# Sparse attention with a chosen expert: a rebuilt first batch, another list order, and products of a constant tile in TensorE's waits

## The chip, the cores and the metric

The kernel runs on one core of a Trainium2 chip. The metric is the device time of one execution in microseconds (us); lower is better. A core's engines are TensorE (PE in the profile, its weight loads PEld), VectorE (DVE), ScalarE (ACT), GpSimd (POOL) and SyncE (SP). The last two mostly issue transfers here. Every kernel below was checked against the reference, and all were correct.

## The reference

Four batches of 768 positions, 8 heads of 64. Each position attends to the 15 neighbours on either side and to 24 blocks of 32 positions (maximum of k, mean of v). The mean over the attention output chooses one of eight experts for the whole batch, and the batch then goes through that expert alone.

```python
k_sum = k.reshape(B, H, nb, block, D).max(axis=3)
v_sum = v.reshape(B, H, nb, block, D).mean(axis=3)
...   # softmax over [scores inside the window, scores on blocks + log(32)]
attn = np.matmul(a, np.concatenate([v, v_sum], axis=2))
...
pooled = x.mean(axis=1)
e_idx = np.argmax(pooled @ w_gate, axis=1)
h = np.maximum(x[mask] @ w1[e], 0.0)
out[mask] = gate_w[mask, None, None] * (h @ w2[e])
```

So an expert's weights can't be fetched before the last attention product of its batch has gone through the gate.

## The kernel before

A small list scheduler in the kernel's source estimates durations, orders all operations of all batches, and emits each engine's list in that order. Each engine then works through its list in order. The parts that matter:

```python
# three expert banks in PSUM, each a tile of its own
mps_pool = ctx.enter_context(tc.tile_pool(name="mps", bufs=3, space=PS))
...
def mm():                                   # one expert group: 4 products into one bank
    sb["hps"] = mps_pool.tile([128, 512], FP32, name="hps")
    for dt in range(NDT):
        nc.tensor.matmul(sb["hps"][:, 0 : c1 - c0], lhsT=..., rhs=..., start=(dt == 0), stop=(dt == NDT - 1))
def rl():                                   # ScalarE evicts it
    nc.scalar.activation(sb["hT"][:, ft, c0:c1], ps["t"][:, 0 : c1 - c0], ACT.Relu)
```

```python
def halo_v(b, hs):        # neighbour rows of v, copied inside the chip
    vb = vblks[b % 2]
    if b > 0:             # batch 0 loads these 16 rows from memory instead
        nc.sync.dma_start(vb[0:16, 1:NJ, hs, :], vb[64:80, 0 : NJ - 1, hs, :])
    nc.sync.dma_start(vb[80:96, 0 : NJ - 1, hs, :], vb[16:32, 1:NJ, hs, :])
...
for j in range(NJ):       # block sums of v, read from rows 0 to 79
    nc.tensor.matmul(ps[0:32, 0 : n * D], lhsT=bind[:, j, :], rhs=vblks[b % 2][0:80, j, hs, 0:D], ...)
...                       # then VectorE copies them out and SyncE broadcasts them into rows 96 to 119
for hh in range(2):       # probabilities times v: 12 products of 120 rows
    for jj in range(NH):
        nc.tensor.matmul(ops[...], lhsT=aT[0:NR, hh, ...], rhs=vb[0:NR, j, 2 * pr + hh, :], start=True, stop=True)
```

Two one-column copies on GpSimd ("tokens"), which wait for loads of v, hold back the later loads of q and k.

The softmax here doesn't subtract the row's maximum and nothing guards it: scores larger than these inputs give would overflow.

## Time and profile before

| | before |
|---|---|
| time, median of 3 runs | 198.6 us (198.41 to 201.48) |
| gate product of batch 0, 1, 2, 3 | 43.8, 77.5, 121.7, 159.8 us |
| first expert product | 59.2 us |
| last expert product ends | 196.0 us |
| eviction, store and end | 3.8 us |

The rows split the span into stages. From 59.2 to 196.0 us TensorE is busy 124 of 136.8 us. Before that, the time is set by when the first gate product can run. The lines that show this stand in the prediction.

### The profile page before, as it was taken

Reading aid. Unit: us, or ns where it says so; the run is one execution under the profiler, and the core shown is the slowest. Engines: PE = TensorE matmul, PEld = TensorE weight load, DVE = VectorE, ACT = ScalarE, POOL = GpSimd, SP = SyncE. Lnnn points to the kernel's source line nnn. Section 1 sums busy time; section 2 is a strip of 40 time slices with the busy share of each in tenths; the row PEclk is TensorE's granted clock in tenths of the full one; section 3 lists DMA queues with packets and bytes.
Section 4 is the critical chain, followed back from the end, with each engine's and each line's share of the span. In section 5 each row is a group of like instructions: output and inputs, shape, how many; then the busy total and the mean of one; then the engine's idle time right before and its main releaser. Section 6 shows DMA issues by size and latency. Waiting matters only on the chain.

```text
span 199.8 us, 4547 instructions
## 1 busy us (share of the span) xinstructions
PE 160.0 (80%) x1902; PEld 93.0 (47%) x1924; DVE 100.7 (50%) x209; ACT 95.7 (48%) x182; POOL 42.4 (21%) x67
## 2 busy tenths in 40 slices
PE   0342877765989799999999899958999995399992
PEld 0231666544365475434556454334556542156440
DVE  5472488599386789311898781563797210000000
ACT  2203267442057676513778736223888642056431
POOL 6126934007420520911025001100000030000000
PEclk9999999999999999999999999996999999579999
DMA  5999999915999999899999957799200039980142
GB/s 86 210 179 156 178 227 214 166 32 80 178 179 225 198 175 151 138 191 257 267 239 191 184 78 208 147 218 242 39 3 0 3 111 229 260 137 0 56 153 111
DMA packets 28689, 30.45 MB, mean 152 GB/s; under 512 B 9756, under 2 KB 22812, under 8 KB 28572
## 3 DMA queue, kind: packets, MB, share of 16 engines
q0 software_dynamic: 14800, 19.40, 59.6%
q1 hardware_dynamic: 13868, 10.75, 21.3%
q8 instruction: 15, 0.25, 0.5%
q14 instruction: 6, 0.05, 0.1%
HBM read 36.06 MB, written 6.29 MB: 212 GB/s over the span
## 4 chain that ended last, share of the span: by engine, by line
PE 55%; DMA 25%; DVE 6%; SPq 4%; issue 3%; ACT 3%; POOL 2%; POOLq 1%; ACTq 0%
PE hps L726 23%; PE hps L760 15%; DMA w_sb<-in_moe_w_dram 11%; DMA v_f<-in_v_dram 7%; DMA q_nat<-in_q_dram 4%; PE ops L359 4%; PE sc L464 4%; SPq L216 3%; PE ops L497 3%; DMA vblk<-vblk 2%; PE kps L407 2%; PE tps L521 2%; PE tps L432 2%; DVE kT L426 1%; DVE xs L511 1%
## 5 line engine op out<-in xcount | busy, mean ns | idle before, releaser
L726 PE MATMUL hps<-xT_b,w_sb 128*128 128x256 bf16 (+1 forms) x239 | 50.3, 343 | 9.3 <-DMA w_sb<-in_moe_w_dram 7.9
L760 PE MATMUL hps<-w_sb,hT_sb 128*128 128x512 bf16 x187 | 43.4, 380 | 0.3
L741 ACT ACTIVATE hT_sb<-hps 128x512 bf16<-128x512 f32 x64 | 29.8, 490 | 23.4 <-PE hps L726 22.5
L726 PEld LDWEIGHTS <-w_sb 128*128 128x128 bf16 x256 | 23.3, 102 | 24.1 <-DMA w_sb<-in_moe_w_dram 7.9
L475 ACT ACTIVATE aT<-sc 128x768 bf16<-128x768 f32 x32 | 25.9, 809 | 15.7 <-PE sc L464 15.6
L770 ACT ACTIVATE o_sb<-hps,gcol 128x512 f32<-128x512 f32 x24 | 16.5, 687 | 28.2 <-PE hps L760 16.4
L760 PEld LDWEIGHTS <-hT_sb 128*128 128x128 bf16 x192 | 18.0, 98 | 20.5 <-issue 0.9
L213 POOL DMA_DIRECT2D v_f<-in_v_dram x24 | 18.0, 761 | 36.4 <-DMA w_sb<-in_moe_w_dram 26.0
L359 PE MATMUL ops<-vblk,bind 80*32 80x512 bf16 (+1 forms) x60 | 16.3, 445 | 6.0 <-DVE vblk L299 6.0
L479 DVE TENSOR_TENSOR aT<-aT,mask 120x768 bf16<-120x768 bf16 x32 | 17.6, 552 | 4.6 <-ACT aT L475 4.4
L426 DVE COPY kT<-kps 128x1152 bf16<-128x1152 bf16 x12 | 16.2, 1349 | 6.3 <-PE kps L407 6.3
L665 POOL DMA_DIRECT2D w_sb<-in_moe_w_dram x5 | 3.8, 753 | 72.3 <-PE hps L760 51.4
L299 DVE CAST vblk<-v_f 80x1536 bf16<-80x1536 f32 x16 | 14.9, 951 | 7.7 <-DMA v_f<-in_v_dram 7.7
L511 DVE TENSOR_TENSOR xs<-ops,rv 128x384 bf16<-128x384 f32 x32 | 17.8, 558 | 1.1
L407 PE MATMUL kps<-identb,k_nat 96*64 96x96 bf16 x256 | 11.3, 249 | 8.5 <-DMA k_nat<-in_k_dram 7.2
L497 PE MATMUL ops<-vblk,aT 120*64 120x65 bf16 x384 | 13.7, 211 | 4.9 <-DVE xs L511 2.0
L529 ACT ACTIVATE xT_b<-tps 128x768 bf16<-128x768 bf16 x16 | 12.9, 809 | 8.9 <-PE tps L521 8.8
L497 PEld LDWEIGHTS <-aT 120*64 120x64 bf16 x384 | 10.0, 122 | 12.9 <-issue 5.0
L464 PE MATMUL sc<-qT,kT 64*128 64x64 bf16 x384 | 13.1, 210 | 2.9 <-ACT kT L456 1.2
L446 DVE TENSOR_REDUCE kmx<-kT 128x24 bf16<-128x768 bf16 x16 | 15.2, 948 | 0.1
L407 PEld LDWEIGHTS <-k_nat 96*64 96x64 bf16 x256 | 9.2, 139 | 10.6 <-DMA k_nat<-in_k_dram 7.2
L464 PEld LDWEIGHTS <-kT 64*128 64x128 bf16 x384 | 9.2, 105 | 10.0 <-issue 6.4
(55 smaller groups left out, 113.8 us busy)
## 6 DMA issues: line engine op xcount, KB each, us to landing
w_sb<-in_moe_w_dram POOLq DMA_DIRECT2D x7, 1024.0 KB, 15.8
out_dram<-o_sb SPq DMA_DIRECT2D x24, 256.0 KB, 5.1
v_f<-in_v_dram POOLq DMA_DIRECT2D x24, 192.0 KB, 11.2
k_nat<-in_k_dram POOLq DMA_DIRECT2D x6, 384.0 KB, 10.3
q_nat<-in_q_dram POOLq DMA_DIRECT2D x6, 384.0 KB, 11.3
v_f<-in_v_dram SPq DMA_DIRECT2D x7, 240.0 KB, 7.2
vblk<-vblk SPq DMA_DIRECT2D x6, 178.8 KB, 6.2
w_sb<-in_moe_w_dram POOLq DMA_DIRECT2D x2, 512.0 KB, 9.4
```

Source lines behind the costliest of these rows:

```text
L213: nc.gpsimd.dma_start(v_f[16:80, :, h, :], v[b, h].rearrange("(j p) d -> p j d", p=QB))
L359: nc.tensor.matmul(ps[0:32, 0 : n * D], lhsT=bind[:, j, :], rhs=vblks[b % 2][0:80, j, hs, 0:D], start=(j == 0), stop=(j == NJ - 1),)
L407: nc.tensor.transpose(kps[hh * D : (hh + 1) * D, g, 2 : 2 + SP], qk_nat[b][1][:, 2 * pr + hh, g, :], identb[0:SP, 0:SP],)
L426: nc.vector.tensor_copy(kdst, win)
L464: nc.tensor.matmul(sc[:, hh, jj * QB : (jj + 1) * QB], lhsT=sb["kT"][pr][rs, j, :], rhs=sb["qT"][pr][rs, j, :], start=True, stop=True, til ...
L475: nc.scalar.activation(aT, sb["sc"][:, :, 0 : NH * QB], ACT.Exp, scale=SCALE)
L479: nc.vector.tensor_tensor(out=aT[0:NR], in0=aT[0:NR], in1=mask[:, hf * NH : (hf + 1) * NH, :] .rearrange("p j c -> p (j c)") .unsqueeze(1) ...
L497: nc.tensor.matmul(ops[(j % 2) * QB : (j % 2 + 1) * QB, hh, jj // 2, :], lhsT=aT[0:NR, hh, jj * QB : (jj + 1) * QB], rhs=vb[0:NR, j, 2 * p ...
L511: nc.vector.tensor_tensor(out=sb["xs"][pr][:, hf * NS : (hf + 1) * NS, :, :].rearrange("p s h d -> p h s d"), in0=ops[:, :, :, 0:D], in1=r ...
L726: nc.tensor.matmul(sb["hps"][:, 0 : c1 - c0], lhsT=sb["w1"][:, dt, ft * 128 : (ft + 1) * 128], rhs=sb["xT"][:, dt, c0:c1], start=(dt == 0) ...
L741: nc.scalar.activation(sb["hT"][:, ft, c0:c1], ps["t"][:, 0 : c1 - c0], ACT.Relu)
L760: nc.tensor.matmul(ps["t"], lhsT=sb["hT"][:, ft, st * 128 : (st + 1) * 128], rhs=sb["w2"][:, ft, :], start=(ft == 0), stop=(ft == NFT - 1),)
```

## The change

Its intent: bring the first batch's data in earlier and in the order of need, drop the broadcast of its block sums, let the two halves of a head pair use different PSUM banks, keep TensorE's clock up by products of a constant tile in early and long waits, and order the list so that later batches' attention runs ahead of experts. Its core (set-up steps, estimated durations, the first batch's explicit sequence and a rule of the list scheduler, that a result of the same engine counts as ready once issued, are left out):

```diff
-    mps_pool = ctx.enter_context(tc.tile_pool(name="mps", bufs=3, space=PS))
+    mps_pool = ctx.enter_context(tc.tile_pool(name="mps", bufs=1, space=PS))
+    kbank = kps_pool.tile([128, 1024], BF16, name="kbank")     # k transposes, and a spare part
+    idle_ps = kbank[:, G * (SP + 4) : 1024].bitcast(FP32)
+    idle_in = const_pool.tile([128, 128], BF16, name="idle_in")
+    mps = mps_pool.tile([128, 3, 512], FP32, name="mps")
...
-        if b > 0:
-            nc.sync.dma_start(vb[0:16, 1:NJ, hs, :], vb[64:80, 0 : NJ - 1, hs, :])
+        nc.sync.dma_start(vb[0:16, 1:NJ, hs, :], vb[64:80, 0 : NJ - 1, hs, :])
...
-    tk = add("POOL", 0.2, [v_loads[2], bind_setup], lambda: nc.gpsimd.tensor_copy(tok[:, 0:1], ...))
...                      # tokens gone; v loads 2 to 7 on GpSimd's queue, between those of q and k
...
+            if second(pr, hf):                 # batch 0, second half of a pair
+                sc = mps[:, 0:2, :]
+            else:
+                sc = sc_pool.tile([128, 2, 512], FP32, name="sc")
...
+            if second(pr, hf):
+                ops = mps[:, 2, :]
...
+                    if b == 0 and jj % 2 == 1:    # block sums as an extra product of 24 rows
+                        nc.tensor.matmul(ops[:, hh, jj // 2, :], lhsT=aT[KW:NR, hh, (jj - 1) * QB : (jj + 1) * QB],
+                            rhs=vs0[KW:NR, 2 * pr + hh, :], start=False, stop=True, tile_position=(KW, 0))
...
-                sb["hps"] = mps_pool.tile([128, 512], FP32, name="hps")
+            ps = {"t": mps[:, len(sch.tags.get("mps", [])) % 3, :]}
...                      # list order
+    DELAY = {"PE": 0.9, "DVE": 0.6, "ACT": 0.6}
-                    elif (
-                        start + op["dur"] <= pick[0] + 0.1
-                        or (start < pick[0] and tail[pick[1]["n"]] - tail[op["n"]] < self.URGENT)
+                    elif start < pick[0] and (
+                        start + op["dur"] <= pick[0] + self.DELAY.get(eng, 0.1)
+                        or tail[pick[1]["n"]] - tail[op["n"]] < self.URGENT
-        sch.prio = 40.0 if b == 0 else 0.0
+        sch.prio = 40.0 if b == 0 else 8.0
...                      # constant products in planned waits
+                if t < self.FILL_TO:
+                    self.fill(int((idle - 0.4) / (0.1 if t < 8.0 else 0.08)))
+                else:
+                    self.fill(int((idle - 1.2) / 0.08))
+    def fill(n):
+        for _ in range(n):
+            nc.tensor.matmul(idle_ps, lhsT=idle_in, rhs=idle_in[:, 0 : idle_ps.shape[1]], start=True, stop=True)
```

## The prediction

> **What bounds the kernel now.** I read first the slices of the page, then the chain that ended last, then the same time cut into stages, then TensorE's own timeline. The slices of the kernel before:
>
> ```profile
> PE   0342877765989799999999899958999995399992
> PEclk9999999999999999999999999996999999579999
> DMA  5999999915999999899999957799200039980142
> ```
>
> One character is 5 us. TensorE is poorly filled for the first ten or eleven slices and nearly full from 60 us on, with two holes near 132 and 170 us. No other engine comes near this: VectorE is busy 50% and ScalarE 48% of the span. The stages (columns: stretch, its length, busy us and count on PE, weight loads, DVE, ACT, POOL, then clock, DMA share, GB/s):
>
> ```profile
> 7.20:43.90 36.70, 23.37 (x392) 17.85 (x392) 22.31 (x41) 15.60 (x24) 13.27 (x20) 1.00 1.05 172
> 43.90:59.20 15.30, 12.40 (x161) 7.86 (x161) 11.17 (x21) 3.96 (x8) 7.48 (x10) 1.00 0.88 133
> 59.20:132.70 73.50, 69.47 (x855) 38.39 (x868) 45.26 (x90) 41.81 (x85) 15.59 (x21) 1.00 1.01 191
> 132.70:135.40 2.70, 0.26 (x13) 0.23 (x8) 2.45 (x4) 0.64 (x1) 0.00 (x0) 1.00 1.12 189
> 135.40:167.50 32.10, 31.77 (x384) 17.13 (x388) 15.41 (x35) 20.34 (x41) 1.65 (x2) 0.95 0.35 78
> 167.50:172.90 5.40, 0.00 (x1) 0.00 (x0) 0.16 (x1) 0.69 (x1) 0.00 (x0) 0.76 1.09 243
> 172.90:196.00 23.10, 22.69 (x109) 11.50 (x112) 0.00 (x0) 10.51 (x21) 0.00 (x0) 0.91 0.40 100
> ```
>
> So there are three regimes. Up to 43.9 us (the first batch's attention, ending in its gate) no engine is full: a chain of small steps, held by loads, sets the time. From the gate to 59.2 us, the first expert product, the chosen expert's weights are fetched (issued at 46.15 us, first landing 8.5 us later at best). After 59.2 us TensorE is the bound, but for two waits in which the weights of batches 2 and 3 are not there. The chain of waits says the same:
>
> ```profile
> 13.01 4.94 DMA vblk<-vblk
> ...
> 124.18 10.97 DMA w_sb<-in_moe_w_dram
> ...
> 162.22 10.66 DMA w_sb<-in_moe_w_dram
> ```
>
> The first is the copy of the neighbour rows of v inside the chip; the others are the weight fetches, of which TensorE hides all but 2.46 and 5.43 us. Within the first stage the first product of probabilities and v starts at 24.3 us, though the first scores are exponentiated at 15.9: it waits for casts of v (which wait for v's load until 19.37), for neighbour rows, for block sums and, since TensorE's list is in order, for whatever stands before it. Finally TensorE's timeline:
>
> ```profile
> 49.60 5.30 PE L359 MATMUL ops<-vblk,bind 80*32 80x512 bf16 x12
> 58.35 0.50 PE L464 MATMUL sc<-qT,kT 64*128 64x64 bf16 x12
> 61.33 0.35 PE L464 MATMUL sc<-qT,kT 64*128 64x64 bf16 x12
> 126.39 2.81 PE L359 MATMUL ops<-vblk,bind 80*32 80x512 bf16 x12
> 172.93 0.61 PE L726 MATMUL hps<-xT_b,w_sb 128*128 128x512 bf16 x1 [5.43 <-DMA w_sb<-in_moe_w_dram]
> ```
>
> The same twelve block-sum products take 5.30 us early and 2.81 late. TensorE is slow from the start until about 61 us, although the clock row prints 9 there; that row cannot be trusted for the first 60 us, the durations can.
>
> **What the Trainium skill says.** "TensorE: Matmul & The Clock Gate", Part 1 (the HAM clock gate): the array starts at half clock, gets the full clock after some 3.4 us of activity and loses it after about as much idleness. The trace agrees: 5.30 against 2.81 us, and granted clock 0.76 in and 0.91 after the 5.4 us wait. The same page, Part 4 (PE-mode transpose), says transposes don't count as activity in the usual way. The trace fits: from 23 to 58 us TensorE was some three quarters busy with transposes, small attention products and 32-column block sums and never sped up; two microseconds of 128x128 expert products did it. So a filler of 128x128 weights is the right kind. "DMA: Bandwidth & Descriptors", Queues, rings and completion order: each DMA engine takes turns between the queues packet by packet. This fits the neighbour rows' 7.0 us to landing for 89 KB while v loads were running; I therefore don't count that copy as short after the change.
>
> **The change, part by part.**
>
> *Loads of the first batch.* The v loads are no longer 80 rows with 16 read twice, and only two of eight stay on the Sync queue; the rest follow on GpSimd's queue in the order of need, and GpSimd's two token waits (4.34 and 4.90 us) are gone. Issue costs about 0.75 us for a v load and 1.3 for a pair's q and k (GpSimd timeline), so six v loads, four pairs and the setup end near 1.5+6x0.75+4x1.3+3.0=14 us instead of 19 (last pair of the first batch issued at 18.0 to 19.3). The bytes as the profile counts them are 3.15 MB; at the observed 190 GB/s from 3.5 us that is 20 us, with neighbour rows and landing about 23 us (estimate).
>
> *Block sums.* Their broadcast into all blocks (146 KB twice, on the path at 35.8 us: 1.39 us of wait for it) is dropped for batch 0. Instead 3 extra products per head and half, 6 per group of 12: 48 in all, at about 25 to 45 ns (12 products take 0.31 to 0.54) under 2.2 us of TensorE, mostly in gaps.
>
> *Second PSUM set.* The second half of each pair uses expert banks that are idle then. Before, each product-normalise step took about 1.6 us (35.83, 37.49, 39.06, 40.73), one after another. Now it should come down toward VectorE's 0.75.
>
> *When is gate 0?* Three estimates. Data: last q and k at 23, then transposes 0.5, kT copy 1.13, maxima 0.95, spread 0.45, scores 0.3, exp 0.81, mask 0.56, product 0.5, normalise 0.75, half two 0.8, transpose 0.4, copy with sum 1.0: 8.15, with about 0.1 per hand-over 9.5, so 32.5. VectorE: first product near 18.5 (v cast 11, neighbour rows 7), then 8 normalisations 6.0, four masks 2.2, two pairs' copies and maxima 3.0, cast and sums 1.3 = 12.5, with some stalls 33. Second v group: cast near 20, rows 26.5, then four steps of 1 us and 1.7 for the end: 32. I take 33 against 43.9: 11 us.
>
> *Warm filler.* Warm, the first batch's TensorE groups fall from 0.85 to 0.5, 0.50 to 0.35, 0.54 to 0.38 us. About half lies on the path; this is inside the estimate. After the gate the 512-column block sums and seven transposes go warm (2.5 + 7x0.33 + some scores = about 5 us). If weights are issued at 33+2.4 and land after 8.5 to 9.5 us, the first expert product comes at 45 instead of 59.2: 14.2 us, of which 11 are the gate's and 3 the TensorE work that no longer stands in front.
>
> *List order.* Attention of later batches gets priority 8 us over the experts. At gate 3 (160 us) only 7.1 us of expert 2's products were left to cover the fetch of 10.7 (issue 2 us later), so 5.43 stayed open. Eight more microseconds held back cover that, and likewise the 2.46. I count 6 of 7.9, as an earlier attention also needs its own loads earlier. Filler and absence of waits save the half-speed start after each: the hidden products 172.93 to 185.42 take 12.5 where warm ones (32 of 0.216 and 32 of 0.135) would be 11.2, 1.3 us; about 1.5 at 135; say 2.8 together. Removed waits and cold starts do not overlap with anything but each other.
>
> Sum: 14.2+6+2.8=23; a further 1 for small waits in the list; 198.6-24=174.6. Check from the other side: 45 + (196.0-59.2-8-3.5) = 170.3 as last product, + 3.8 as before for eviction and store, + 1.5 (measured 201.35 against span 199.8) = 175.6, less a share of the profiled run's 2.8 us excess over the fast runs.
>
> **Rivals.**
> - *The DMA takes the place:* loads that came after the gate's idle patch (slice of 32 GB/s at 40 to 45 us) now crowd; batch 1's loads stand in GpSimd's queue before the first weights. For it: DMA share near 1.1 until 100 us. Against it: 112 to 123, 140 to 160 and 176 to 190 us are nearly empty. It would hold the first expert product near 52: 181 us.
> - *The filler doesn't warm, or gets in the way:* it runs before a real product in an in-order engine and is counted from planned gaps. Then gate 0 is at about 37 and the rest 3 us worse: 181 us.
> - *Weights waits stay* because attention cannot run ahead of VectorE's 26 us per batch (four pairs of 1.35+0.55+0.95+2x0.55+2x0.75, four casts of 0.95, sums 0.7): 180 us.
> - *Everything better:* gate near 29 and a tight list: 168 us.
>
> **Range and chances.** One rival alone gives 180 to 181, two 187. I predict 174.5, 167 to 183; faster by over 2% (under 194.6) 0.97.
>
> **What would show it.** Gate products at 33 (30 to 37) and first expert product at 45; score groups at 0.35 in the first 40 us, early 512-column block sums at 2.8; no TensorE wait over 1 us on weights of batches 2 and 3; from first expert product to last about 126 us. Wrong if the first weights land after 50, if early groups stay at 0.50, or if that last stretch remains 135.

## The result

| | before, same rounds | after |
|---|---|---|
| median of 5 runs | 201.48 us (198.41 to 210.71) | 248.4 us (244.32 to 249.17) |
| ratio of fast runs | | 1.232 (95%: 1.223 to 1.240) |
| gate products | 43.8, 77.5, 121.7, 159.8 us | 59.9, 114.3, 154.0, 191.1 us |
| first expert product | 59.2 us | 79.4 us |
| last expert product ends | 196.0 us | 242.5 us |

Ratios here and below are the mean time of one kernel's fast runs over that of the other's fast runs of the same rounds, so they are not quite the ratio of the medians. Executions over 1.5% slower than the fastest of the same kernel are left out of the means. Both profiled executions lay above their kernel's fast runs, by a similar share: 201.35 us (before, fast from 198.41) and 249.17 us (after, fast runs 243.88 to 245.27; the first of these is a sixth run, not among the median's five). So the stages are compared like with like.

The change was predicted to save 24 us and cost 46. By stages: up to the end of the first gate product 16.3 us more (60.2 against 43.9), from there to the first expert product 3.9 more (19.2 against 15.3), among the experts 26.4 more (163.2 against 136.8), and 0.5 at the end.

The slices of the page for the kernel after; one character is a fortieth of the span, here 6.2 us:

```profile
PE   5509989998679867999996798998798776655862
PEclk9965555555555897799999999999999999999999
DMA  6999891000699995015899999799200499100123
```

TensorE, poorly filled in the first 60 us before, is now full there from 20 us on. Its granted clock is at half for 60 us, and it is loosest (5 to 8) in the last 60 us, where before it had been nearly full apart from one wait for weights. The stages, in the columns of the prediction's stage table:

```profile
60.20:79.40 19.20, 15.09 (x173) 10.18 (x171) 11.13 (x20) 2.86 (x7) 7.49 (x10) 0.50 0.93 145
79.40:242.60 163.20, 131.03 (x1412) 69.37 (x1408) 65.21 (x130) 75.03 (x149) 17.20 (x23) 0.97 0.63 122
20.00:60.00 40.00, 38.22 (x453) 27.66 (x452) 17.53 (x36) 15.33 (x23) 4.32 (x6) 0.50 0.47 82
```

The last row is the reading that turns the case: from 20 to 60 us TensorE is busy 38.2 of 40 us at half clock, while the DMA engines idle half the time. Data is not what is missing; the array's own work is. The second row says the opposite of the expert stage: it is 32 us longer than TensorE's work in it, so there it waits. For what, is in TensorE's waits (columns: what waited for what; us in total, times, longest):

```profile
PE mps L837 <- ACT hT_sb L848: 18.0, 37, 0.7
PE ops L405 <- DMA vblk<-vblk: 7.9, 2, 6.7
PE mps L866 <- ACT o_sb L876: 7.4, 10, 0.8
...
PE kbank L949 <- DVE kT L476: 4.1, 2, 2.7
PE kbank L949 <- DVE kbank L248: 2.5, 1, 2.5
PE mps L837 <- ACT o_sb L876: 2.3, 3, 1.3
```

The first, third and last of these lines (with one more wait of 1.0 us of the same kind, 28.7 us together) are expert products that wait for ScalarE's evictions of the group before. In the kernel before no such wait appears: its expert products wait only for weights and, for 0.9 us, for issue. The second line is the block sums waiting for the neighbour rows; the fourth and fifth are constant products, which wait themselves and hold up what stands behind them. The chain that ended last, after (start, duration, what), shows the first kind in the row:

```profile
237.89 1.90 PE mps L866 x8
...
239.86 0.70 ACT o_sb L876
240.56 0.04 issue
240.60 1.90 PE mps L866 x8
```

Product group, eviction, product group: one output tile every 2.71 us (240.60 - 237.89), although three banks are rotated through. Before, the same stretch of TensorE's timeline is one unbroken row, 8 products in 1.79 us:

```profile
185.42 10.52 PE L760 MATMUL hps<-w_sb,hT_sb 128*128 128x512 bf16 x47
```

Finally TensorE's timeline after, to be read against the one in the prediction (start, length, line, tiles, count, and in brackets the idle time before):

```profile
2.53 4.27 PE L949 MATMUL kbank<-idle_in 128*128 128x112 bf16 x44 [2.53 <-DVE kbank L248]
6.72 0.55 PE L457 MATMUL kbank<-identb,k_nat 96*64 96x96 bf16 x16
...
18.92 2.51 PE L405 MATMUL ops<-vblk,bind 80*32 80x256 bf16 x11 [6.74 <-DMA vblk<-vblk]
21.36 0.85 PE L457 MATMUL kbank<-identb,k_nat 96*64 96x96 bf16 x16
...
28.76 0.27 PE L556 MATMUL mps<-vblk,aT 96*64 96x65 bf16 x2
28.96 0.23 PE L564 MATMUL mps<-vs,aT 24*128 24x65 bf16 x1
29.12 0.27 PE L556 MATMUL mps<-vblk,aT 96*64 96x65 bf16 x2
...
72.35 5.30 PE L405 MATMUL ops<-vblk,bind 80*32 80x512 bf16 x12
```

The constant products at 2.5 us do warm the array: the next 16 transposes take 0.55 us. Then the block sums wait 6.74 us for the neighbour rows, and from there the same transposes take 0.85. The products of probabilities and v come in trios of two and one, 0.36 us from one trio to the next (29.12 - 28.76), so a half takes six trios, 2.16 us. Before, at the same half clock, a half was:

```profile
24.32 0.53 PE L497 MATMUL ops<-vblk,aT 120*64 120x65 bf16 x12
```

And at 72 us the block sums of batch 1 still take the cold 5.30 us.

### The profile page after: what moved, and what is told of

Its sections match the earlier page's. It is cut to its first block, busy times and chain, and to the rows that moved or that the text cites. A ratio compares the mean times of both kernels' runs of the same rounds, so it can differ in the third digit from the quotient of the medians.

```text
span 246.9 us, 5000 instructions
## 1 busy us (share of the span) xinstructions
PE 192.8 (78%) x2146; PEld 114.8 (46%) x2146; DVE 103.7 (42%) x211; ACT 101.7 (41%) x185; POOL 46.0 (19%) x70
## 5 line engine op out<-in xcount | busy, mean ns | idle before, releaser
L837 PE MATMUL mps<-xT_b,w_sb 128*128 128x512 bf16 (+1 forms) x256 | 52.4, 338 | 20.5 <-ACT hT_sb L848 18.0
L866 PE MATMUL mps<-w_sb,hT_sb 128*128 128x512 bf16 x192 | 45.3, 379 | 8.4 <-ACT o_sb L876 7.4
L848 ACT ACTIVATE hT_sb<-mps 128x512 bf16<-128x512 f32 (+1 forms) x64 | 29.4, 489 | 41.9 <-PE mps L837 41.8
L876 ACT ACTIVATE o_sb<-mps,gcol 128x512 f32<-128x512 f32 x24 | 16.4, 687 | 41.3 <-PE mps L866 31.6
L949 PE MATMUL kbank<-idle_in 128*128 128x112 bf16 x174 | 16.7, 277 | 7.5 <-DVE kT L476 4.1
L556 PEld LDWEIGHTS <-aT 120*64 120x64 bf16 (+1 forms) x384 | 13.1, 118 | 13.5 <-issue 6.2
L949 PEld LDWEIGHTS <-idle_in 128*128 128x128 bf16 x174 | 14.4, 132 | 8.1 <-issue 6.0
L556 PE MATMUL ops<-vblk,aT 120*64 120x65 bf16 (+1 forms) x336 | 15.8, 212 | 2.2 <-DMA vblk<-vsb 1.3
L476 DVE COPY kT<-kbank 128x1152 bf16<-128x1152 bf16 x12 | 16.2, 1346 | 2.0 <-PE kbank L457 1.9
L405 PEld LDWEIGHTS <-bind 80*32 80x32 bf16 x60 | 6.9, 122 | 17.1 <-issue 13.2
## 6 DMA issues: line engine op xcount, KB each, us to landing
w_sb<-in_moe_w_dram POOLq DMA_DIRECT2D x7, 1024.0 KB, 15.3
```

Source lines behind the costliest of these rows:

```text
L405: nc.tensor.matmul(ps[p0 : p0 + 32, 0 : n * D], lhsT=bind[:, j, :], rhs=vblks[b % 2][0:80, j, hs, 0:D], start=(j == 0), stop=(j == NJ - 1),)
L476: nc.vector.tensor_copy(kdst, win)
L556: nc.tensor.matmul(ops[(j % 2) * QB : (j % 2 + 1) * QB, hh, jj // 2, :], lhsT=aT[0:rows, hh, jj * QB : (jj + 1) * QB], rhs=vb[0:rows, j, 2 ...
L837: nc.tensor.matmul(ps["t"][:, 0 : c1 - c0], lhsT=sb["w1"][:, dt, ft * 128 : (ft + 1) * 128], rhs=sb["xT"][:, dt, c0:c1], start=(dt == 0), ...
L866: nc.tensor.matmul(ps["t"], lhsT=sb["hT"][:, ft, st * 128 : (st + 1) * 128], rhs=sb["w2"][:, ft, :], start=(ft == 0), stop=(ft == NFT - 1),)
L876: nc.scalar.activation(ps["o"], ps["t"], ACT.Copy, scale=sb["gcol"][:, 0:1])
```

## The experiments

The theory after reading the traces has four parts. (1) The expert banks have become parts of one tile, and so an eviction of one bank stands between products into the others. (2) The 24-row products between 96-row products cost far more than their own length. (3) The block sums wait for the copy of neighbour rows, which now writes rows that they read. (4) The constant products take time on a TensorE that is full. The rivals: the transfers that start earlier crowd out the small copies and that is the whole early loss; and, for the expert stage, the half clock or the new list order.

All outputs are right. Five calls on the chip were made. The median of the kernel before was 201.4, 201.6, 199.7, 202.6 and 203.0 us in them.

### a_banks: three tiles for the expert banks, all else as after

```diff
-    mps = mps_pool.tile([128, 3, 512], FP32, name="mps")
+    mps = [mps_pool.tile([128, 512], FP32, name=f"mps{i}") for i in range(3)]
-                sc = mps[:, 0:2, :]
+                sc = mps[0:2]            # exp of such a half then runs once per head
-            ps = {"t": mps[:, len(sch.tags["mps"]) % 3, :]}
+            ps = {"t": mps[len(sch.tags["mps"]) % 3]}
```

> The changed kernel with the three expert PSUM banks as three separate tiles again (the second score set of batch 0 takes two of them, its exponential in two instructions). Theory 1: since the three banks are one tile, every access to it is put in order of issue, and TensorE waits 28.7 us for ScalarE's evictions; these waits go, 244.3 falls to 216 to 222. Theory 2: the half-speed array of the first 82 us is the loss and the waits only fill slack: it stays over 237.

Measured: 224.97 us (222.17 to 226.95), ratio 1.118 (1.102 to 1.134) against 1.232 of after, which is 22.6 us ((1.232 - 1.118) x 198.7, the mean of the fast runs of the kernel before in the third call, used for all such conversions here; from unrounded ratios). The gate stays at 60.1 and the first expert product at 79.7; the last one ends at 221.6 instead of 242.5. The expert waits for ScalarE are gone, and TensorE's longest expert waits are for weights again:

```profile
PE mps L845 <- DMA w_sb<-in_moe_w_dram: 7.2, 2, 4.4
```

So part 1 carries most of the loss of the expert stage: it falls from 163.2 to 141.9 us (136.8 before), at the same list order and the same early stage.

### b_onetile: the kernel before, with its three expert banks made one tile

```diff
-    mps_pool = ctx.enter_context(tc.tile_pool(name="mps", bufs=3, space=PS))
+    mps_pool = ctx.enter_context(tc.tile_pool(name="mps", bufs=1, space=PS))
+    mps_all = mps_pool.tile([128, 3, 512], FP32, name="mps")     # used as mps_all[:, n % 3, :]
```

> The kernel before, with nothing changed but its three expert PSUM banks made one tile of three banks. Theory 1: TensorE waits for each eviction as in the changed kernel, 198.5 rises to 222 to 230. Theory 2 (only the first batch is to blame): below 203.

Measured: 231.57 us (230.32 to 235.29), ratio 1.156 (1.141 to 1.171), a little above what was expected. The banks, the rotation and the arithmetic are as before; only the tile that they belong to differs. TensorE's waits are those of the kernel after, nearly to the count:

```profile
PE mps L733 <- ACT hT_sb L748: 18.5, 36, 0.7
PE mps L767 <- ACT o_sb L777: 9.4, 12, 1.0
```

With a_banks this settles part 1 from both sides: put in, it costs 31 us; taken out, it gives 22.6. Neither the clock nor the list order is needed for it.

### a_sums: the neighbour rows of batch 0 are copied after the block sums

```diff
-            hl = add("SP", 1.2, cs, lambda b=b, hs=hs: halo_v(b, hs), dma=0.8 * len(gs))
+            hl = None        # for b > 0 as before the edit
...              # after the block sums' products, o_vs:
+            if b == 0:
+                hl = add("SP", 1.2, [o_vs], lambda b=b, hs=hs: halo_v(b, hs), dma=0.8 * len(gs))
```

> The changed kernel with the neighbour-row copy of batch 0 put after the block sums in program order, so that the sums needn't wait for it. Theory 3: the waits of 6.7 and 1.2 us of the block sums go, first scores at about 14 us instead of 22, total 234 to 238, and if the array stays warm for lack of the long idle stretch, as low as 226. Rival: the first product of probabilities and v then waits for the later copy, total above 241.

Measured: 242.2 us (240.5 to 247.48), ratio 1.206 (1.190 to 1.222): 5.1 us less than after, fewer than expected. The gate comes at 53.4 instead of 59.9. The sums' wait is gone, but products of probabilities and v now wait 2.3 us for those rows. Part 3 stands, at 5 to 6.5 us rather than the 7.9 us of its waits.

### a_extras: the 24-row products of a half grouped behind its twelve

A half then opens its bank with one product of a zero tile, because all that follows accumulates.

```diff
+            if b == 0:
+                nc.tensor.matmul(ops..., lhsT=nought, rhs=..., start=True, stop=False)   # 96x128 zeros, 390 columns
-                    if b == 0 and jj % 2 == 1:
+            if b == 0:
+                for hh in range(2):
+                    for jj in range(1, NH, 2):        # the six 24-row products, after the twelve
```

> The changed kernel with the six extra block products of each half moved behind its twelve ordinary ones instead of one after every two; one product with zero weights (96x128 by 390 columns) opens the accumulation. Theory 4: the alternation between full-height and 24-row products costs, 12+6 products take 2.15 us because each switch costs about 0.1 us; grouped they take 0.4+0.54+0.35 us, 8 halves save some 7 us, total 235 to 239. Rival: an extra product itself costs 0.23 us wherever it stands: 2.15 plus 0.4 us, total 245 to 249.

Measured: 239.79 us (238.52 to 241.97), ratio 1.198 (1.181 to 1.215), 6.7 us better than after; gate at 53.3. Its TensorE timeline:

```profile
38.65 0.51 PE L556 MATMUL mps<-aT,nought 96*128 96x390 bf16 x1
39.09 0.54 PE L566 MATMUL mps<-vblk,aT 96*64 96x65 bf16 x12
39.56 0.51 PE L576 MATMUL mps<-vs,aT 24*128 24x65 bf16 x6
```

A half now takes 1.36 us (38.65 to 40.01, where the next group starts), although it has one product more. Eight halves times 2.16 - 1.36 is 6.4 us, and the gate moved by 6.6: in this stage TensorE's length is the gate's time, nearly one for one. "TensorEngine Tiling (Array Packing)" in the Trainium skill, Key Properties under Tiling Modes, says that changing the tiling mode drains TensorE. These traces fit that: products of 96 rows into 64 columns and of 24 rows into 128, taken in turn, cost 0.80 us more per half than in two groups with an opener. Without the opener the two groups take 0.92 us (39.09 to 40.01), so each of the twelve switches costs about 0.10 us (estimate: 2.16 - 0.92 over 12). I had not used that page in the prediction. A rival, that a product which adds to a result just written must wait for it, was not tested apart. The block sums speak against it: each adds to the one before, and at half clock they cost 0.89 ns a column (before, 2.72 us for 12 of 256 columns), while the constant products, which add to nothing, cost 0.87 (after, 4.27 us for 44 of 112).

### c_bse: all three repairs together

The edits of a_banks, a_sums and a_extras in one kernel.

> The changed kernel with the three repairs together (three PSUM tiles, block sums ahead of the neighbour rows, extra products grouped). Theory: the three causes are separate and add up: 244 less about 22, 4 and 6 gives 212, range 206 to 216, gate of batch 0 near 46. If they overlap (the same slow array behind all of them), it stays over 218.

Measured: 213.28 us (209.37 to 216.06), ratio 1.055 (1.033 to 1.077), gate at 47.2, first expert product at 67.2. The parts add: 22.6 + 5.1 + 6.7 = 34.4 us alone, 35 us together ((1.232 - 1.055) x 198.7). The intervals of the ratios leave some 4 to 5 us either way on each of these numbers, so they agree, but no more closely than that. Some 11 us above the kernel before remain.

### c_bsb and c_bsb_nofill: no extra products at all, with and without the constant ones

Banks and sums repaired; the broadcast of the block sums restored for batch 0, the 24-row products gone. The second kernel has, in addition:

```diff
-        for _ in range(n):
+        for _ in range(0):          # fill()
```

> As the run before it, but with the block sums of batch 0 broadcast again and no extra products at all. Theory 4: the extra products are a loss in any form, as TensorE is the bound of the changed first batch: gate near 42, total 200 to 207. Rival: the broadcast's transfer, 146 KB twice, comes back as a wait: total as c_bse or worse.

> As c_bsb, with the constant products left out. Theory 5: they warm the array only while they run and cost TensorE about 10 us in the first 70 us, part of it waits for the kT copies whose PSUM bank they share: 2 to 6 us faster than c_bsb. Rival (the intent of the change): without them the array is slower for longer, 2 to 5 us slower than c_bsb.

Measured: c_bsb 207.77 us (203.23 to 208.24, one fast run, hence no ratio), gate at 44.1, first expert product at 61.1. c_bsb_nofill 202.2 us (200.77 to 202.37), ratio 1.011 (1.002 to 1.021), gate at 44.0, first expert product at 58.0. The constant products don't move the gate here, and the first expert product comes 3.1 us sooner without them. Part 4 stands in sign. Its size is loose: fast with fast it is 1.3 us, from c_bsb's one fast run and the other's mean of 201.9; the 5.6 us of the medians set slow runs of c_bsb against fast ones.

### c_bse_nofill and c_bse_mfill: the three repairs without constant products, and with few

The first removes the constant products from c_bse. The second keeps them only for planned waits of over 1.2 us, and writes them into an expert bank, so that they wait for no copy of k.

```diff
-    FILL_TO = 45.0
+    FILL_TO = 0.0
-                idle_ps, lhsT=idle_in, ...
+                t[:, 0:112], lhsT=idle_in, ...     # t: the next expert bank
```

> All three repairs and no constant products. Theory 5 (the constant products take TensorE's time in a first batch that TensorE bounds): as with the broadcast, 5 us or more below c_bse, 200 to 206. And as no broadcast is waited for (7.2 us in c_bsb_nofill), the gate of batch 0 should come at 37 to 41, ahead of the kernel before. Rival: the grouped extra products cost as much as the broadcast's wait: gate at 44 or later.

> All three repairs, constant products only in planned waits of over 1.2 us, early too, and written to an expert bank instead of the bank of the transposed k. Theory 5: what costs is the filling of small gaps and the shared bank; this is at or up to 3 us below c_bse_nofill. Rival: any filling costs: above c_bse_nofill by 3 us or more.

Measured: c_bse_nofill 201.6 us (198.4 to 206.14), ratio 1.005 (0.995 to 1.015); c_bse_mfill 201.51 us (200.16 to 202.37), ratio 1.014 (1.007 to 1.021). Against c_bse the constant products cost (1.055 - 1.005) x 198.7 = 10 us, with some 5 us either way (two fast runs each). Sparing ones give nothing that shows in the time, though the gate of c_bse_mfill comes at 46.5. But the gate of c_bse_nofill came at 49.0 and not at the 37 to 41 that I expected: a miss. One of its waits is 5.1 us for the neighbour rows. So with all repairs made, the first batch is still no earlier than before, and something else holds it.

### b_list, b_list5, b_list_again: the kernel before with the new list order alone

```diff
+    DELAY = {"PE": 0.9, "DVE": 0.6, "ACT": 0.6}
...              # the list-order hunks of the change, and priority 8 for later batches' attention; nothing else
```

> The kernel before with the change of the list order alone (delays allowed on each engine, same-engine results ready at issue, 8 us of priority for later attentions). The prediction's step: the two waits for weights, 2.5 and 5.4 us, shrink and with them the slow starts: 190 to 195. Rival: attention can't run ahead, waits stay: 197 to 201.

> The kernel before with the list order alone again, for an interval. The order's gain is real: 190 to 195, 2 to 4% faster than before. Rival: only the one fast run was good: within 1%.

> The list order alone on the same chip, as the measure for d_holdbc1: 2.5 to 4% below the kernel before.

Measured: 195.03 us (190.55 to 200.79) in the second, 195.52 (191.99 to 198.07) in the third, 195.9 (194.77 to 198.58) in the fifth, where the kernel before had medians of 201.6, 199.7 and 203.0. Only the third has enough fast runs for an interval: 0.973 (0.964 to 0.981), 5.4 us; in the second b_list had one fast run, in the fifth the kernel before had one. TensorE's waits for weights, in the kernel before and in b_list5:

```profile
PE hps L726 <- DMA w_sb<-in_moe_w_dram: 7.9, 2, 5.4
```

```profile
PE hps L731 <- DMA w_sb<-in_moe_w_dram: 3.4, 1, 3.4
```

One wait of two is gone, 4.5 us of 7.9. In b_list5 the experts last from 58.5 to 190.8 us, 132.3 instead of 136.8: 4.5 of the 5.2 us by which the two profiled spans differ (199.8 and 194.6). The list order is the part of the change that helps, and alone it beats both kernels.

### b_list_mfill: the same, with constant products in planned waits of over 1.2 us

> As b_list5 with constant products in planned waits of over 1.2 us, written to an expert bank. If warming helps where nothing else runs, the 512-column sums of batch 1 take 2.8 instead of 5.3 us and the last expert starts at full clock: 186 to 191. Rival: small attention products let the array cool again before these: no gain over b_list5, or 1 to 3 us more.

Measured: 195.78 us (191.08 to 201.13), ratio 0.962 (0.955 to 0.970), which rests on two fast runs, 191.08 and 191.27; the other four lie between 194.66 and 201.13. The batch-1 block sums still take 5.30 us and the first transposes 0.85. Its median is that of b_list5, and a gain over it is not shown.

### d_hold1, d_hold2, d_holdbc, d_holdbc1: who gets the transfers

The change also removed what held transfers back: batch 1's first loads are issued at 14.1 us instead of 19.3. The rival of crowding says that the neighbour-row copies (89 KB inside the chip) then land late. In the first batch they took a median of 7.0 us to landing in the kernel before, 6.7 in the kernel after, so no later there, and 9.6 in c_bse_nofill. These four put a token on GpSimd in front of batch 1's loads.

```diff
+            for g in [0]:                     # d_hold2, d_holdbc: [0, 1]
+                order_pool[:] = [add("POOL", 0.2, [v_ready[0][g][0]],    # neighbour rows of group g
+                    lambda g=g: nc.gpsimd.tensor_copy(tok[:, g : g + 1], vblks[0][0:16, NJ - 1, HW * g + HW - 1, 0:1]),
+                    after=order_pool)]
```

d_hold1 and d_hold2 are c_bse_nofill with it, d_holdbc and d_holdbc1 are c_bsb_nofill with it.

> c_bse_nofill with the loads of batch 1 held back on GpSimd's queue until the neighbour rows of batch 0's first four heads have landed. Theory 6: the removed token waits kept other loads off the neighbour rows; held back again, these land in under 8 us instead of 9.6, the 5.1 us wait of the first product shrinks to 3 or less and the gate comes at 44 to 46; total 196 to 200. Rival: batch 0's own loads crowd them as much: gate as before at 49.

> As d_hold1, held until the neighbour rows of both groups of heads have landed. Theory 6: as d_hold1 and the second group's rows land in about 4 us: gate at 42 to 44; but batch 1's data come later, so the total is 195 to 200. Rival: batch 1's later data cost more than that: total above 202.

> c_bsb_nofill (broadcast block sums, no extra products) with batch 1's loads held until both groups' neighbour rows of batch 0 have landed. Theory 6: the broadcast waits of 7.2 us shrink by about half and the gate comes at 39 to 42; total 194 to 199. Rival: no change in those waits.

> As d_holdbc, but batch 1's loads are held only until the first group's neighbour rows have landed (released at about 21 us instead of 27). If the early stage is a matter of which transfers go first, this is the compromise: gate at 38 to 42, gate of batch 1 no later than 86, total 192 to 197, beside or ahead of the list order alone. Rival: either the small transfers or batch 1's data are still late: total over 198.

| kernel | held for | us, median | gate 0 | gate 1 |
|---|---|---|---|---|
| d_hold1 | first group | 201.04 (196.92 to 201.74) | 45.7 | 86.2 |
| d_hold2 | both groups | 216.3 (212.41 to 219.0) | 41.8 | 100.0 |
| d_holdbc | both groups | 210.08 (207.92 to 216.32) | 35.4 | 91.5 |
| d_holdbc1 | first group | 203.18 (201.19 to 204.93) | 45.9 | 85.8 |

Crowding is real: held for both groups, the neighbour rows land in 4.7 us (d_hold2) instead of 9.6, and without fillers and extra products, the gate comes at 35.4 (d_holdbc) instead of 44.0 us (c_bsb_nofill). That is nearly the 33 of the prediction, and the first expert product comes at 52.7. Yet the kernel is some 4 us slower than c_bsb_nofill: its two fast runs are 1.030 of the mean of the kernel before's fast runs in their call (208.3 and 202.1 us), c_bsb_nofill's 1.011 (the medians, 8 us apart, mix slow runs with fast). For batch 1's data come later, and with them its gate (91.5 instead of 83.1), all later gates and the weights. The totals expected of d_hold2 and d_holdbc were missed. TensorE's waits in d_holdbc:

```profile
PE mps L846 <- DMA w_sb<-in_moe_w_dram: 11.4, 4, 5.3
```

Holding them for one group brings no gain that is shown: d_hold1 has its gate 3.3 us earlier than c_bse_nofill and nearly its median (its one fast run, 196.92, lies below the 201.3 to 202.97 of the kernel before in that call, but it is one run), and in d_holdbc1, which I expected to have its gate at 38 to 42, the wait moved to the broadcast of the block sums (9.6 us, once). The early loads are needed by batch 1, and the early copies by batch 0.

## Why the prediction was wrong

**What held.** TensorE's list is the bound once the experts run, in the kernel before and in those with the banks repaired. GpSimd had issued the first batch's loads at 14.1 us (14 predicted). The clock row of the kernel before is not to be trusted early on: 16 transposes take the cold 0.85 us where it prints 9. A gate near the predicted 33 us was possible, at 35.4 in d_holdbc, but only with the extra and the constant products taken out, banks and sums repaired, and batch 1's loads held back. Constant products can warm the array: 0.55 us per 16 transposes at 6.7 us.

**What it didn't allow for.** None of its rivals was a loss, and all three of its signs of being wrong came: the first weights land after 60 us (50 was the limit), early score groups stay at 0.50 us, and the last stretch is 163.2 us, which is worse than remaining at 135. One reading was off, without bearing on the sum: from 112 to 123 us the DMA engines of the kernel before are busy 75% of the time, not nearly idle.

**"Second PSUM set" failed, and is the largest term.** The prediction treated it as a gain for the first batch: normalise steps closer together. That gain exists where the banks are separate: in c_bsb_nofill the last four products of probabilities and v start at 38.33 to 41.07 us, 0.91 us a step, where it was 1.63. The prediction passed over the line of the diff that makes one tile of three banks. With one tile, TensorE's next group waits for the eviction of the one before, whatever bank that was in: 28.7 us of such waits, 22.6 us of time by a_banks, 31 us when put into the kernel before. The prediction's expected 126 us from first to last expert product became 163.2.

**"48 in all ... under 2.2 us of TensorE, mostly in gaps" failed twice.** The size: a half went from 0.53 us to 2.16, so eight halves cost 13 us more. A product's length alone was counted, not what switching between the two shapes costs. The place: there were no gaps, TensorE was busy 38.2 of 40 us. Grouping gave 6.7 us back.

**"Block sums" left out a wait.** The prediction saw the neighbour-row copy grow to a part that had been loaded from memory, but not that the sums read those rows. TensorE waited 6.7 and 1.2 us, with everything that stood behind, and a_sums gave 5.1 us of time.

**"Warm filler" failed.** By the clock and by the lengths, the array was at half speed from 15 to about 80 us, although 53 fillers (6.0 us) ran between 25 and 60. The 174 fillers of the kernel after hold TensorE for 16.7 us in all; taking them out gained 10 us in c_bse, and about 1 in c_bsb by the little that can be compared there. Rival 2 of the prediction, "doesn't warm, or gets in the way", named this, fillers in an in-order list placed by planned gaps included, and gave it 3 us and a later gate. What it missed is that the gaps are not there when TensorE is full, and that a filler itself waits for the copies of k out of the bank that it shares (4.1 us). Nor does the same filler warm the array each time. In a_extras the same 44 products at the start leave the transposes behind them cold, at 0.85 us instead of 0.55:

```profile
2.62 4.27 PE L961 MATMUL kbank<-idle_in 128*128 128x112 bf16 x44 [2.62 <-DVE kbank L250]
6.82 0.85 PE L459 MATMUL kbank<-identb,k_nat 96*64 96x96 bf16 x16
```

Why this array stayed cold at 95% busy is open.

**"List order" held in direction.** 6 of 7.9 us of weight waits were counted; alone it removed 4.5, and the time fell by 5.4 us (b_list5). The warm starts, 2.8 us, were not measured apart. In the whole change the gain isn't visible: a_banks still waits 7.2 us for weights and c_bsb_nofill 6.1. Why those waits come back when the first batch is rebuilt was not settled.

**"The DMA takes the place" held as a mechanism, not as the bound.** In the kernel after, TensorE's own list kept the gate at 60. Once repaired, the transfers decide: the same loads can serve the first gate or the second.

**The sum.** After cost (1.232 - 1) x 198.7 = 46 us. One tile 22.6, block sums 5.1 and shape switches 6.7 by their single repairs, 35 for the three together, and the constant products 10 (each with some 5 us either way) leave c_bse_nofill at 0.9 us above the kernel before. That kernel still contains the list order, worth 5.4 us alone. So the rest of the rebuilt first batch costs about 6 us (estimate, if the two simply add). In c_bse_nofill it is an expert stage that starts at 63.8 instead of 58.5 us; in c_bsb_nofill it starts at 58.0 but lasts 137 us instead of 132.3.

## What to carry to other kernels

When a change merges buffers, ask who writes and who reads every part of the merged one: rotating banks keep engines apart only if each bank is a tile of its own. Before adding small products or fillers "in gaps", look whether TensorE will have gaps after the change, and count what switching shapes costs, not the product's own length. Moving transfers earlier is not a gain in itself: follow the small copies and the next batch's data that share the engines with them, and try the parts of a bundled change one at a time, since here one part alone was worth 5 us, and the bundle around it cost 46.

## What the Trainium skill lacked or had wrong

- "Perfetto Trace Analysis", Matmuls under Optimizing Tensor Performance, advises that groups rotate through PSUM banks so that evacuation overlaps the next group's products. It lacks that in the kernel's source the banks have to be separate tiles: three banks rotated through as parts of one tile gave 28.7 us of waits for evictions, one output tile per 2.71 us instead of 1.79.
- "TensorEngine Tiling (Array Packing)", Key Properties, says that a mode change drains TensorE, which the traces fit, but gives no cost. Here, at half clock, twelve 96-row products with six 24-row ones between them took 2.16 us, and 1.36 us in two groups with an opener of about 0.44; the twelve alone 0.54.
- "TensorE: Matmul & The Clock Gate", Part 1, ties the full clock to activity. Here 38.2 us of activity in 40 stayed at half clock (16 transposes 0.85 us; twelve block sums still 5.30 us at 72 us), with 6.0 us of constant 128-row products among it. What kind of activity counts, beyond its note on transposes, isn't there.
- None of the pages that I read has a figure for a small copy inside the chip among large loads: the 89 KB copies of neighbour rows took a median of 9.6 us to land with batch 1's loads beside them (c_bse_nofill), and 4.7 with those held back (d_hold2).
